# A fused attention and MLP kernel: batch 0 computed in whole tiles, and batch 2 loaded in transpose order by groups

## The chip, the cores and the metric

The kernel runs on one NeuronCore of a Trainium2 chip. Times are device microseconds (us) of one execution. A kernel is timed in several runs, on the same chip as the kernel before. The main number before the change is 419.73 us, median of 3 runs.

Five engines matter. TensorE (PE) multiplies matrices, ScalarE (ACT) does the exponentials, reciprocals and GELU, VectorE (DVE) adds and copies, GpSimd (POOL) issues all loads from DRAM that cast to fp16, and SyncE (SP) issues the stores and the transposing DMAs.

## The reference

```python
# q, k, v: (8 batches, 12 heads, 448 rows, 64), float32
scores = q @ k.T / sqrt(64)
m = max(scores)
e = exp(scores - m)
attn = e / (sum(e) + exp(-m) + 1e-9)         # "softmax off by one"
x = (attn @ v) laid out as (3584 tokens, 768)
h = x @ w_in                                  # 768 x 2048
out = gelu_exact(h) @ w_out                   # 2048 x 768
```

The kernel calls x @ w_in "layer 1" and the last product "layer 2".

## The kernel before

Twelve heads make three groups of four, so there are 24 groups numbered s = 0 to 23; batch b has groups 3b to 3b+2. Per group there are seven key chunks of scores, exponentials into `et`, the value products, and the denominators: VectorE sums the seven tiles into `ksum`, and four matmuls with a matrix of ones add that up.

q and k must be transposed for the scores. Batches 0 and 1 are turned by TensorE. From batch 2 on a transposing DMA does it, issued by SyncE. It needs its source in chunk order. For batch 2 VectorE makes that order; for batches 3 and up the load itself writes it, in short runs:

```python
def load_ordered(name, b):                    # POOL, one DMA per half, group and head pair
    for x in range(2):
        for g in range(NG):
            for e in range(2):
                nc.gpsimd.dma_start(out=by_chunks(name, b)[half[x], g, :, e, :], in_=dram(name, b)[x][:, g, e])

def order_and_turn(name, b, g):
    o = order_pool.tile([P, J, 2, D], FP16, name="order" + name)
    for e in range(2):
        nc.vector.tensor_copy(out=o[:, :, e, :], in_=natural(name, b)[:, g, e])
    nc.sync.dma_start_transpose(out=turned(name, b)[:, g], in_=o...)
```

Batch 0 goes through nine narrow passes (three slices of the queries by three groups), with narrow pieces of layer 1 between them; then come a burst of GELUs and the attention of batch 1 beside layer 2 of batch 0. At the end of that part stands this:

```python
    for name in "qk":
        alloc_raw(name, 3)
        nc.vector.memset(raw[name, 3][:, 0:1], 0.0)   # one column, on VectorE
        load_ordered(name, 3)                         # POOL: must wait for that memset
```

The memset writes into the tile that the load fills, so the load of batch 3 cannot be issued before VectorE comes to this place in its own program.

The steady cycle of a batch, cut:

```python
for b in range(1, B - 1):
    s = NG * (b + 1)
    values(s - 1); gap_after_values(s - 1, 2); next_three(s)
    ...            # 16 layer 1 chunks of batch b beside group s, with GELU
    ...            # loads of later batches
    s += 1; next_three(s); gap(3); last_one(s); gap(1 + b % 2); values(s); gap_after_values(s, 2 + b % 2)
    s += 1; next_three(s); gap(2); last_one(s); gap(2)       # gap: layer 2 items
```

In layer 2 of batch 0 the stores of the first half of the columns are kept back, because the second half of w_out comes late, and all go out with the first store of the second half:

```python
    if b == 0 and nh == 0:
        held.append(lambda: store([(nc.sync, osb, x, w)]))
    else:
        store([(nc.sync, osb, x, w)])
        for f in held:
            f()
```

The softmax here doesn't subtract the row's maximum and nothing guards it: scores larger than these inputs give would overflow.

Of the kernel before, what the change touches and what calls it, by code (L numbers as in the profile page):

```python
# [9 lines left out]
FP32 = mybir.dt.float32  # L10
# [9 lines left out]
def kernel(  # L20
# [14 lines left out]
    P = 128  # L35
# [7 lines left out]
    JA = 4  # L43
    NBURST = 8
# [16 lines left out]
    order_pool = ctx.enter_context(tc.tile_pool(name="order_pool", bufs=3))  # L61
# [56 lines left out]
    def load_ordered(name, b):  # L118
        if (name, b) not in raw:
            alloc_raw(name, b)  # L120
        for x in range(2):
            for g in range(NG):
                for e in range(2):
                    nc.gpsimd.dma_start(  # L124
                        out=by_chunks(name, b)[half[x], g, :, e, :], in_=dram(name, b)[x][:, g, e])
# [11 lines left out]
    def load_w_out(nh, i, n):  # L137
# [7 lines left out]
    PASS = [(0, 2, [(0, 4), (4, 7)]), (2, 4, [(0, 4), (4, 7)]),  # L145
            (4, 7, [(0, 2), (2, 4), (4, 6), (6, 7)])]
# [6 lines left out]
    KA = 4  # L153
    QF = PASS[0][1]
    pieces = (("q", 0, QF), ("k", 0, KA), ("k", KA, J))
# [12 lines left out]
    nc.gpsimd.memset(gt_even[:, 0:4, :], 0.0)  # L168
# [5 lines left out]
    for g in (1, 2):  # L174
        load_group("q", 0, g, 0, JA)
        load_group("k", 0, g)
        load_group("v", 0, g - 1)
    load_group("v", 0, 2)
    if QF < JA:
        load_group("q", 0, 0, QF, JA)  # L180
    load_all("q", 0, JA, J)
    for i in range(4):
        load_w_in(i, 4)
    load_group("q", 1, 0)
    load_group("k", 1, 0)
    for i in range(2):
        load_w_out(0, i, 2)
    load_group("q", 1, 1)
    load_group("k", 1, 1)
    load_all("v", 1)  # L190
    for i in range(2):
        load_w_out(1, i, 4)
    load_group("q", 1, 2)
    load_group("k", 1, 2)
    for i in range(2, 4):
        load_w_out(1, i, 4)
# [26 lines left out]
    def order_and_turn(name, b, g):  # L223
        o = order_pool.tile([P, J, 2, D], FP16, name="order" + name)
        for e in range(2):
            nc.vector.tensor_copy(out=o[:, :, e, :], in_=natural(name, b)[:, g, e])
        nc.sync.dma_start_transpose(
            out=turned(name, b)[:, g], in_=o.rearrange("p j e d -> p (j e d)"))
# [31 lines left out]
    def den_mms(dst, ksum):  # L260
        for x in range(2):
            for e in range(2):
                nc.tensor.matmul(  # L263
                    dst[half[e], x], ones[half[x]], ksum[half[x], e], start=True, stop=True)
# [22 lines left out]
    def exps(s, j, st):  # L287
        if j == 0:
            et_t[s] = et_pool.tile([P, J, 2, S], FP16, name="et")
            sum_t[s] = sum_pool.tile([P, 1024], FP16, name="ksum")  # L290
        et = et_t[s]
        exp_scores(et[:, j], st[:, :, 0:S])
        if j:
            ksum = sum_t[s][:, 0:2 * S].rearrange("p (e s) -> p e s", e=2)
            adds.append(lambda: add(ksum, et[:, 0] if j == 1 else ksum, et[:, j]))
# [5 lines left out]
    def values(s):  # L301
        val_t[s], den_t[s] = new_st(), new_st()
        st = new_st() if s + 1 < B * NG else None
        value_mms(val_t[s][:, :, 0:S], s, et_t.pop(s))
        den_mms(den_t[s][:, :, 0:S], sum_t.pop(s)[:, 0:2 * S].rearrange("p (e s) -> p e s", e=2))
# [123 lines left out]
    NUNIT = len(PASS) * NG  # L429
    QH = JA * D  # L430
    hv = {}

    def width(i):
        j0, j1, tiles = PASS[i // NG]
        return (j1 - j0) * D

    def h_scores(i, *ts):
        j0, j1, tiles = PASS[i // NG]
        n = width(i)
        made = []  # L440
        for t in ts:
            st = new_st()
            for jj, j in enumerate(range(*tiles[t])):
                score_mms(st[:, :, jj * n:(jj + 1) * n], i % NG, j, j0, j1)
            made.append((i, t, st))
        return made

    def h_exps(made):
        for i, t, st in made:
            n = width(i)  # L450
            k0, k1 = PASS[i // NG][2][t]
            if t == 0:
                et_t[i] = et_pool.tile([P, J, 2, S], FP16, name="et").rearrange(
                    "p j e s -> p (j e s)")[:, 0:J * 2 * n].rearrange(
                        "p (j e s) -> p j e s", j=J, e=2)
                sum_t[i] = sum_pool.tile([P, 1024], FP16, name="ksum")
            exp_scores(
                et_t[i][:, k0:k1].rearrange("p j e s -> p e j s"),
                st[:, :, 0:(k1 - k0) * n].rearrange("p e (j s) -> p e j s", j=k1 - k0))

    def h_sums(i, j):
        n = width(i)
        e = et_t[i].rearrange("p j e s -> p (j e s)")
        acc = sum_t[i][:, 0:4 * n]
        if j == 2:
            add(acc, e[:, 0:4 * n], e[:, 4 * n:8 * n])
        elif j == 4:
            add(acc, acc, e[:, 8 * n:12 * n])
            add(acc[:, 0:2 * n], acc[:, 0:2 * n], acc[:, 2 * n:4 * n])
        else:  # L470
            add(acc[:, 0:2 * n], acc[:, 0:2 * n], e[:, 12 * n:14 * n])

    def h_values(i):
        n = width(i)
        hv[i] = new_st()
        value_mms(hv[i][:, :, 0:n], i % NG, et_t.pop(i))
        den_mms(
            hv[i][:, :, QH:QH + n],
            sum_t.pop(i)[:, 0:2 * n].rearrange("p (e s) -> p e s", e=2))

    def h_reciprocal(i):
        n = width(i)
        rec_t[i] = rec_pool.tile([P, 2, S], FP32, name="rec")
        reciprocal(rec_t[i][:, :, 0:n], hv[i][:, :, QH:QH + n])

    def h_normalize(i):
        n, g, c0 = width(i), i % NG, PASS[i // NG][0] * D
        nc.vector.tensor_tensor(
            out=xt_of(0)[:, 2 * g:2 * g + 2, c0:c0 + n], in0=hv.pop(i)[:, :, 0:n],
            in1=rec_t.pop(i)[:, :, 0:n], op=ALU.mult)  # L490

    def h_layer1(f0, f1, c0, c1, w):
        ph = ps_bank.tile([P, 512 // w, w], FP32, name="bank")
        for f in range(f0, f1):
            for m in range(MCH):
                nc.tensor.matmul(  # L496
                    ph[:, f - f0, 0:c1 - c0], w_in_sb[:, m, f * P:(f + 1) * P],
                    xt_t[0][:, m, c0:c1], start=m == 0, stop=m == MCH - 1)
        return ph

    FPH = NBURST // 2 * S // QH
    QP = 2 * D

    def early1(pas, k):
        i, part = divmod(k, 2)
        f0, f1 = (0, FPH // 2 + 1) if part == 0 else (FPH // 2 + 1, FPH)
        ph = h_layer1(i * FPH + f0, i * FPH + f1, pas * QP, (pas + 1) * QP, QP)
        if (pas, part) == (0, 0):
            h_t[i] = h_pool.tile([P, NBURST // 2 * S], FP32, name=f"hbuf{i}")
        nc.vector.tensor_copy(  # L510
            out=h_t[i].rearrange("p (f s) -> p f s", s=QH)[:, f0:f1, pas * QP:(pas + 1) * QP],
            in_=ph[:, 0:f1 - f0])

    def window0():
        load_table(SET_GELU)
        for i in range(2):
            gelu(gt_even[:, i * FPH:(i + 1) * FPH, 0:QH],
                 h_t[i].rearrange("p (f s) -> p f s", s=QH))
        f0 = 2 * FPH
        gelu(gt_even[:, f0:, 0:QH], h_layer1(f0, FCH, 0, QH, QH))  # L520
        w = NFULL - QH
        for f in range(0, FCH, 2):
            if f in (8, 12):
                turn_on_pe("q" if f == 8 else "k", 1, 0)
            ph = h_layer1(f, f + 2, QH, S, QH)
            gelu(gt_even[:, f:f + 2, QH:], ph[:, :, 0:w])
            gelu(gt_odd[:, f:f + 2, 0:D], ph[:, :, w:w + D])
        load_table(SET_LN_EXP)
        l2.extend(layer2_items(0))


    nc.vector.tensor_copy(out=natural("q", 0)[:, 0, :, 0:QF, :], in_=first_rows["q", 0])
    nc.scalar.copy(out=natural("k", 0)[:, 0, :, 0:KA, :], in_=first_rows["k", 0])
    turn_on_pe("q", 0, 0, 0, QF)
    turn_on_pe("k", 0, 0, 0, KA, tile_=ps_st.tile([P, J, P], FP16, name="st"), copy=nc.scalar.copy)
    h_exps(h_scores(0, 0))
    nc.vector.tensor_copy(out=natural("k", 0)[:, 0, :, KA:J, :], in_=first_rows["k", KA])
    turn_on_pe("k", 0, 0, KA, J)
    h_exps(h_scores(0, 1))

    def turn_q(g, j0, j1):
        turn_on_pe("q", 0, g, j0, j1)

    def turn_qk(g):
        turn_q(g, 0, JA)
        turn_on_pe("k", 0, g)

    before1 = {
        0: lambda: turn_qk(1),
        1: lambda: turn_qk(2),  # L550
        2: lambda: turn_q(0, 2, JA),
        5: lambda: turn_q(0, JA, J),
    }
    after1 = {
        5: lambda: early1(0, 0),
        6: lambda: turn_q(1, JA, J),
        7: lambda: (turn_q(2, JA, J), early1(1, 0)),
        8: lambda: early1(0, 2),
    }
    after2 = {  # L560
# [193 lines left out]
```

## Time and profile before

| | before |
|---|---|
| median of 3 runs | 419.73 us (419.51 to 419.86) |
| span of the profiled run, mean granted clock | 419.3 us, 0.973 (this run, timed as the others are, took 421.03 us) |
| PE busy | 396.3 us (95%), 3835 matmuls |
| ACT, DVE, POOL busy | 274.4, 188.7, 139.3 us |

PE is busy 95% of the span, so it bounds the kernel as a whole. The prediction below shows where the other 5% and the low clock lie: in the first 90 us.

### The profile page before, as it was taken

What the parts mean: (1) busy time and instruction counts of PE and PEld (TensorE: products, weight loads), DVE (VectorE), ACT (ScalarE), POOL (GpSimd) and SP (SyncE); (2) the same over time, 40 slices, a digit from 0 to 9 for tenths busy, and PEclk for the clock granted to TensorE, in tenths of its full rate; (3) what the DMA queues carried; (4) which work ended last, traced back from release to release, by engine and by line L of the source; (5) the groups of instructions that cost most, each with busy time, mean ns of one, the idle gap of its engine ahead of it and who ended that gap; (6) DMA issues with size and microseconds to landing.
All of it is one profiled execution on the core that took longest, in us unless ns stands there. A gap on an engine that the chain in (4) does not pass through costs nothing.

```text
span 419.3 us, 9164 instructions
## 1 busy us (share of the span) xinstructions
PE 396.3 (95%) x3835; PEld 222.2 (53%) x3835; DVE 188.7 (45%) x339; ACT 274.4 (65%) x378; POOL 139.3 (33%) x209
## 2 busy tenths in 40 slices
PE   6768898889999999999999999999999999999995
PEld 3657774444555455554555455554555455555564
DVE  2747416786335650556335650556235650640021
ACT  4667757786777675867767776867776776854300
POOL 9913545029969968522930200020000000000000
PEclk8659999999999999999999999999999999999999
DMA  8999999269999999939972860149012100120032
GB/s 135 147 203 205 184 201 160 46 127 163 172 155 147 133 164 158 101 78 196 90 64 69 138 106 20 38 85 177 13 29 69 39 0 20 39 57 20 1 78 73
DMA packets 118377, 42.97 MB, mean 102 GB/s; under 512 B 92992, under 2 KB 118336, under 8 KB 118336
## 3 DMA queue, kind: packets, MB, share of 16 engines
q0 software_dynamic: 75424, 22.52, 51.6%
q1 hardware_dynamic: 42320, 19.52, 23.0%
q8 instruction: 30, 0.49, 0.5%
q10 hardware_dynamic: 592, 0.34, 0.3%
q14 instruction: 11, 0.09, 0.1%
HBM read 45.61 MB, written 11.01 MB: 135 GB/s over the span
## 4 chain that ended last, share of the span: by engine, by line
PE 87%; ACT 6%; DVE 2%; POOL 2%; issue 2%; DMA 1%; DVEq 0%; POOLq 0%
PE bank L380 34%; PE bank L340 31%; PE st L256 8%; PE st L247 8%; PE bank L496 4%; ACT et L267 2%; ACT gt_even L330 1%; PE st L263 1%; DMA rawk<-in_k_dram 1%; DVE ksum L270 1%; ACT rec L273 1%; PE bank L216 1%; ACT L69 1%; POOL rawq L106 1%; ACT rec L274 1%
## 5 line engine op out<-in xcount | busy, mean ns | idle before, releaser
L267 ACT ACTIVATE et<-st 128x896 f16<-128x896 f32 (+3 forms) x171 | 143.7, 901 | 35.2 <-PE st L247 35.0
L340 PE MATMUL bank<-xt,w_in_sb 128*128 128x448 f16 x672 | 130.9, 353 | 0.0
L270 DVE TENSOR_TENSOR ksum<-ksum,et 128x896 f16<-128x896 f16 (+2 forms) x123 | 72.3, 588 | 79.8 <-ACT et L267 76.9
L340 PEld LDWEIGHTS <-w_in_sb 128*128 128x128 f16 x672 | 64.3, 98 | 63.8 <-issue 5.9
L380 PE MATMUL bank<-w_out_sb,gt_odd 128*128 128x384 f16 (+1 forms) x528 | 87.0, 322 | 0.0
L380 PEld LDWEIGHTS <-gt_odd 128*128 128x128 f16 x528 | 49.7, 98 | 36.6 <-issue 6.4
L380 PE MATMUL bank<-w_out_sb,gt_even 128*128 128x384 f16 x384 | 66.7, 327 | 1.3 <-DVE tqk L217 1.3
L247 PE MATMUL st<-tqk 64*64 64x448 f16 (+2 forms) x840 | 49.1, 334 | 7.8 <-issue 2.5
L124 POOL DMA_DIRECT2D rawq<-in_q_dram x60 | 42.9, 722 | 37.5 <-issue 25.0
L399 DVE COPY osb<-bank 128x384 f32<-128x384 f32 (+1 forms) x56 | 30.7, 549 | 49.2 <-PE bank L380 49.2
L380 PEld LDWEIGHTS <-gt_even 128*128 128x128 f16 x384 | 35.6, 98 | 30.3 <-issue 7.4
L273 ACT ACTIVATE rec<-st 128x896 f32<-128x896 f32 (+2 forms) x30 | 23.0, 768 | 42.1 <-PE st L263 42.0
L114 POOL DMA_DIRECT2D rawv<-in_v_dram x28 | 17.4, 629 | 84.8 <-PE st L263 75.5
L256 PE MATMUL st<-et,rawv 64*64 64x448 f16 (+2 forms) x840 | 39.8, 330 | 4.1 <-ACT et L267 1.9
L124 POOL DMA_DIRECT2D rawk<-in_k_dram x60 | 42.6, 718 | 0.0
L330 ACT ACTIVATE gt_odd<-bank 128x448 f16<-128x448 f32 (+2 forms) x72 | 29.1, 405 | 18.3 <-PE bank L340 18.3
L350 DVE COPY hbuf<-bank 128x448 f32<-128x448 f32 x48 | 29.9, 623 | 22.7 <-PE bank L340 22.4
L247 PEld LDWEIGHTS <-tqk 64*64 64x64 f16 x840 | 20.9, 115 | 29.0 <-issue 19.4
L321 DVE TENSOR_TENSOR xt<-st,rec 128x896 f16<-128x896 f32 x21 | 22.8, 1086 | 24.5 <-ACT rec L274 24.5
L256 PEld LDWEIGHTS <-rawv 64*64 64x64 f16 x840 | 22.3, 116 | 19.6 <-issue 11.6
L330 ACT ACTIVATE gt_even<-bank 128x384 f16<-128x384 f32 (+2 forms) x33 | 15.3, 467 | 19.3 <-PE bank L340 14.3
L270 DVE TENSOR_TENSOR ksum<-et 128x896 f16<-128x896 f16 (+2 forms) x30 | 17.3, 577 | 21.9 <-ACT et L267 21.8
(44 smaller groups left out, 209.2 us busy)
## 6 DMA issues: line engine op xcount, KB each, us to landing
out_dram<-osb SPq DMA_DIRECT2D x110, 96.0 KB, 2.2
rawv<-in_v_dram POOLq DMA_DIRECT2D x28, 168.0 KB, 5.5
rawq<-in_q_dram POOLq DMA_DIRECT2D x60, 56.0 KB, 3.8
rawk<-in_k_dram POOLq DMA_DIRECT2D x60, 56.0 KB, 3.2
w_in_sb<-in_moe_w_in_dram POOLq DMA_DIRECT2D x4, 768.0 KB, 15.1
rawk<-in_k_dram POOLq DMA_DIRECT2D x16, 112.0 KB, 6.2
w_out_sb<-in_moe_w_out_dram POOLq DMA_DIRECT2D x2, 768.0 KB, 17.3
w_out_sb<-in_moe_w_out_dram POOLq DMA_DIRECT2D x4, 384.0 KB, 8.3
```

Of the source, the lines that this page charges most:

```text
L124: nc.gpsimd.dma_start(out=by_chunks(name, b)[half[x], g, :, e, :], in_=dram(name, b)[x][:, g, e])
L247: nc.tensor.matmul(dst[half[x], e], turned("k", b)[half[e], g, j, half[x]], turned("q", b)[half[e], g, j0:j1, half[x]], start=True, stop=True)
L256: nc.tensor.matmul(dst[half[e], x], natural("v", b)[half[x], g, e, j, :], et[half[x], j, e], start=j == 0, stop=j == J - 1)
L267: nc.scalar.activation(out=out, in_=st, func=AF.Exp, bias=-shift, scale=scale)
L270: nc.vector.tensor_tensor(out=out, in0=a, in1=x, op=ALU.add)
L273: nc.scalar.activation(out=rec, in_=den, func=AF.Ln, bias=math.exp(-shift), scale=1.0)
L321: nc.vector.tensor_tensor(out=xt_of(b)[:, 2 * g:2 * g + 2, :], in0=val_t.pop(s)[:, :, 0:S], in1=rec_t.pop(s), op=ALU.mult)
L330: nc.scalar.activation(out=out, in_=in_, func=AF.Gelu)
L340: nc.tensor.matmul(ph[:, 0:S], w_in_sb[:, m, fc * P:(fc + 1) * P], xt_t[b][:, m, :], start=m == 0, stop=m == MCH - 1)
L350: nc.vector.tensor_copy(out=h_t[i][:, n * S:(n + 1) * S], in_=ph[:, 0:S])
L380: nc.tensor.matmul(po[x][:, 0:w], gt[:, fc, g0:g0 + P], w_out_sb[:, fc, n0 + x:n0 + x + w], start=fc == 0, stop=fc == FCH - 1)
L399: nc.vector.tensor_copy(out=osb[:, 0:w], in_=po[x][:, 0:w])
```

## The change

The diff is shortened, and `...` marks cuts. Intent: do away with the narrow passes. Batch 0's first group runs in mixed tiles as its rows come in, its other two groups as whole tiles, and the steady cycle begins with batch 0, beside the attention of batch 1. Batch 2 comes in chunk order straight from DRAM, group by group, so that VectorE need not order it.

```diff
-    for i in range(NUNIT):                  # the nine narrow passes, 140 lines
-        ...
-    window0()
+    first_scores(0, 0)                      # group 0 by 2 key chunks and by query parts
+    ...
+    values(0); normalize(0); next_three(1); last_one(1)
+    values(1); normalize(1); next_three(2); last_one(2)
...
-    for b in range(1, B - 1):
+    for b in range(B - 1):
...
     def values(s):                          # for s < 3: denominators from all seven tiles
+            den_mms(den_t[s][:, :, 0:S], *(et[:, j] for j in range(J)))
+            value_mms(val_t[s][:, :, 0:S], s, et)
...
-    def order_and_turn(name, b, g):
+    def turn_ordered_group(name, b, g):     # transposing DMA straight from the loaded tile
...
+        if b == 0:                          # after layer 1 of batch 0
+            for name in "qk":
+                load_ordered(name, 2, [0])
+            load_w_out(1, 0, 2)
+            for name in "qk":
+                load_ordered(name, 2, [1])
+            load_w_out(1, 1, 2)
+            for name in "qk":
+                load_ordered(name, 2, [2])
+            load_all("v", 2)
...
         gap(1 + b % 2)
+        if b == 0: turn_ordered_group(q and k, 2, 0)
         values(s)
         gap_after_values(s, 2 + b % 2)
         s += 1
         next_three(s)
         gap(2)
+        if b == 0: turn_ordered_group(q and k, 2, 1)
         last_one(s)
         gap(2)
+        if b == 0:
+            turn_ordered_group(q and k, 2, 2)
+            for name in "qk":
+                load_ordered(name, 3)
-        alloc_raw(name, 3)
-        nc.vector.memset(raw[name, 3][:, 0:1], 0.0)
```

## The prediction

> **What bounds the kernel now.** I read the page's forty slices first, to see where TensorE is not full.
>
> ```profile
> PE   6768898889999999999999999999999999999995
> ACT  4667757786777675867767776867776776854300
> PEclk8659999999999999999999999999999999999999
> DMA  8999999269999999939972860149012100120032
> ```
>
> One slice is 10.5 us. From the tenth slice on PE shows 9 at a full clock; before that it shows 6 to 8, and the granted clock falls to 5 in the third slice. So there are two regimes: a start of some 90 us with holes, and a steady cycle that TensorE bounds. The change rewrites the start. The chain of waits, asked for 84 to 140 us, shows the border:
>
> ```profile
> 89.64 1.52 PE st L256 x28
> 91.15 0.21 PE st L263 x4
> 91.39 0.93 ACT rec L273
> 92.34 0.95 ACT rec L274
> 93.29 1.62 ACT et L267 x2
> ...
> 94.95 0.38 PE st L247 x4
> 95.34 2.38 PE bank L340 x12
> ...
> 102.61 13.72 PE bank L340 x72
> ...
> 137.06 1.45 PE st L256 x28
> ```
>
> Columns are start, duration and work. At 89.64 the value products of group 5 (batch 1's last) start: call it V5. From there both programs run the same code. V5 to V8 is one full cycle of 47.4 us (89.64 to 136.99 in the timeline), nearly all of it PE. Eight such cycles would be 379 us of the 419, so the start can give up at most some 35 to 40 us in all, and most of that is the loading and the first softmax, which nothing can hide. **The whole question is how much earlier V5 comes.**
>
> The groups, shapes kept apart, give the prices:
>
> ```profile
> L267 ACT ACTIVATE et<-st 128x896 f16<-128x896 f32 x147 | 125.2, 915 | 28.8 <-PE st L247 28.7
> L274 ACT ACTIVATE rec<-rec 128x896 f32<-128x896 f32 x21 | 19.9, 950 | 0.7
> L217 DVE COPY tqk<-bank 128x896 f16<-128x896 f16 x8 | 5.0, 622 | 10.5 <-PE bank L216 10.4
> ```
>
> An exponential of 896 columns costs 0.92 us alone and 0.85 in a row (three in 2.54 us in the timeline). In the chain a layer 1 chunk (6 matmuls) is 1.19 us of PE, a layer 2 item (8 matmuls) 1.355, 28 value products 1.45, the scores of one key chunk 0.23, 14 transposes 0.58.
>
> Last, the windows of the clock in the start (columns: stretch, then length, busy PE, PEld, DVE, ACT and POOL, clock, DMA share, GB/s):
>
> ```profile
> 11.26:14.67 3.41, 3.10 (x90) 2.55 (x82) 2.35 (x6) 1.73 (x2) 3.40 (x6) 0.50 1.26 169
> 14.67:18.08 3.41, 1.50 (x72) 1.15 (x68) 2.82 (x9) 3.10 (x6) 3.41 (x6) 1.00 1.06 114
> 18.08:21.50 3.42, 2.73 (x88) 2.23 (x85) 2.04 (x7) 2.91 (x5) 2.37 (x4) 0.50 1.09 163
> 28.30:31.70 3.40, 3.40 (x56) 3.20 (x56) 1.46 (x5) 1.71 (x3) 0.88 (x1) 0.50 1.24 208
> ```
>
> The clock changes at edges 3.41 us apart. A window with 1.5 us of PE work is followed by half clock, one with 3.1 or more by full clock, one with 2.7 at half clock stays there.
>
> **What the Trainium skill says.** "TensorE: Matmul & The Clock Gate", Part 1, has the same 3.4 us free-running window, half clock after an idle one and full after a busy one; the table above agrees, though 1.5 us of short matmuls were not enough to count as busy. "ScalarE: Activation LUTs", What ACT_TABLE_LOAD costs, gives about 1283 ns per table load; the trace has 1.28, and the change keeps the number of switches of batch 0 at two. "DMA: Bandwidth & Descriptors", SWDGE vs HWDGE vs iDMA, says that a cast during a DMA must be issued from GpSimd, so all loads that cast share one issuer: the trace has POOL at 9.99 us busy of 10 in the stretch 10 to 20.
>
> **The change, part by part.** *Removed:* the nine narrow passes over batch 0 with their 276 narrow layer 1 matmuls, the burst of GELUs at 46 to 60 us in which little else ran (ACT 4.98 of 10 us busy in the stretch 50 to 60), and the window after it, 60 to 90 us, in which batch 1's attention was mixed with layer 2 alone and PE still had gaps of 0.6 to 1.3 us. Also 12 ordering copies on VectorE (4.0 us, not on PE's path at all). *Added:* denominators of groups 0 to 2 from seven tiles, not one sum: 24 more matmuls each, 6 x 4 in 6/7 of 1.45 = 1.24 us. *Moved:* 16 layer 1 chunks of batch 0 beside group 3, layer 2 beside groups 4 and 5; two items (12 less 10) are still open at V5, against one before.
>
> *Start to the last exponential of group 0.* The first rows land about as before (same 384 KB ahead of the first scores), so the first exponential starts at about 6.8 (7.13 before). The next two wait: piece k[2:7] has 704 KB ahead of and with it (576 KB landed at 6.39 before), estimate 7.4; cast, transposes at half clock, copy and scores make 9.7. The third tile's scores stand behind the turning of q[4:7]: 10.8. Then they run in a row: 0.9, 0.45, 0.7 x 3, 0.45, and one small wait; the end is about **14.8**.
>
> *Groups 1 and 2.* ACT is the bound. Nine units per group: seven exponentials 7 x 0.85 = 5.95, two of the reciprocal 1.87, one hand-over 0.15: 8.0 us. PE needs only 1.6 + 1.45 + 1.45 + 2 x 0.58 = 5.7 of it at full clock. In group 0's hand-over VectorE copies a turned q ahead of the normalisation, whose score buffer the second tile of the next burst needs: +0.9. So exponentials end at 14.8 + 8.9 + 8.0 = 31.7 if the clock is full. It is hardly full at 14.8: the stretch 7.8 to 14.7 has small matmuls and waits. At half clock 28 + 28 products take 3.2 + 3.2, not 1.5 + 1.5, until the window after the 95% busy one: I put +1.8 on this. The end of group 2's exponentials, A2, is then **33.5**. Later, at 5.7 of 8 us (71%) busy, the clock may drop once more (+1.7) or never have been low.
>
> *A2 to V5.* Laid out in program order by the prices above. Value products, reciprocal and normalisation of group 2 end at A2 + 4.9. In the first eight chunks VectorE is in the way, as two turned copies (1.24), six sums (3.7) and the copies of 0.62 share two banks with PE: values of group 3 start at A2 + 12.3, where the steady cycle has 11.1. Eight more chunks with GELU straight from the bank end at A2 + 28.5. Then 3 scores, 28 transposes and 3 items, 3 scores, 1 item: values of group 4 at A2 + 36.8. Then 4 items, 6 scores and 2 items to V5 at **A2 + 48.2**. A check from the other side: 47.4, less 3 items (13 in a steady cycle, 10 here) 4.1, plus transposes 2.3 and the denominators 1.2, plus 1.3 of VectorE waits, gives 48.1.
>
> *Sum.* V5 at 33.5 + 48.2 = 81.7, against 89.6: 7.9 us earlier. After it there is one item more (1.36 us), which mostly fills PE gaps of 0.79 and 0.42 us that the timeline has at 93 to 95 us: +0.2. 419.7 - 7.9 + 0.2 = 412.0. Without any clock loss it is 410.2; with two it is 413.7.
>
> **Rivals.** *(1) The clock stays full.* The 28 + 28 contiguous products look made for that, and the stretch 74 to 80 us of before held full clock with PE at 4.2 of 6. About 410. *(2) Loads take over.* Up to the last quarter of w_in 7.1 MB (as stored) must land; before moved 6.8 MB by 40 us, so it lands at about 42, and is wanted at A2 + 24 = 57. The values of batch 1 (5.6 MB, about 35 us) are wanted at 46, its second q group (4.7 MB, 30 us) at 37. The second half of w_out stands behind ordered loads that POOL issues at 0.72 us for 56 KB: two groups are 16 of these, 11.5 us, so it should land by 65, and is wanted at about 75. All have 7 us or more. If the order costs what I do not see, 414 to 417. *(3) VectorE or ACT bounds the first cycle*, because layer 2 is missing as filler beside group 3, and the two banks stall: A2 + 50 and 414. *(4) The old narrow passes were worth it*, as they used PE while ACT worked: nothing gained, 418 to 420. Against it: PE was 65 to 71% busy in the first 30 us, much of it at half clock, and had four gaps of 1.1 to 2.5 us there.
>
> **Range and chances.** The sum is 412.0; rival 1 seems somewhat likelier than a second loss, so I take 411.5. Steps A (14.8) and the clock are each uncertain by 2 us, the cycle by 1.5, loads can only add: 407 to 416. Faster by over 2% means below 411.3, almost at my centre: 0.47; within 2% 0.50; slower 0.03.
>
> **What would show it.** Right: a first exponential at about 7, group 0's last at about 15; ACT without long gaps to A2 near 33; V5 near 82; PE full from A2 + 5 on, with short waits on VectorE's copies; the rest unchanged. Wrong: granted clock 1.0 throughout from 11 us (then A2 near 31.5), or 0.5 up to 35 us (A2 at 36); PE waiting for w_in, w_out, rawv or rawq transfers; values of group 3 later than A2 + 14; or a cycle after V5 unlike the old one, which I have assumed the same.

## The result and the profile after

The changed kernel took 415.45 us, median of 4 runs (413.73 to 416.25), against 419.62 us (419.13 to 419.86) for the kernel before, which now has a fourth run. The ratio is 0.9897, 95% interval 0.9864 to 0.9929: within 2%. Ratios here are the mean time of one kernel's runs over that of the other's of the same rounds, so they are not quite the ratio of the medians quoted. Executions over 1.5% slower than the fastest of the same kernel are left out of the means.

The time lies in the predicted range and 4 us above its centre. But the two halves of the sum came out quite differently from the prediction. The slices of the changed kernel:

```profile
PE   7878999949999999999999999999999999999995
ACT  4997776645775787777775786867775776844300
PEclk9999999978999999999999999999999999999999
DMA  8999999999999999759952930258012100220032
```

The granted clock is high from the first slice, in this run: the 5 and 6 of before are gone. PE is at 9 from the fifth slice on. Then there is a 4 in the ninth slice, 83 to 93 us, with the clock at 7 in it and 8 in the next, where the kernel before had 8 and then 9 at a full clock. This is the new hole. Windows of the start, laid 3.40 us long, show the same (columns as in the prediction's windows):

```profile
26.60:30.00 3.40, 2.16 (x34) 0.92 (x34) 1.13 (x2) 3.40 (x6) 2.54 (x4) 1.00 1.26 201
33.40:36.80 3.40, 1.90 (x39) 1.04 (x34) 3.02 (x5) 3.40 (x5) 0.65 (x1) 1.00 1.20 192
```

ACT is busy without a break in these, so it bounds groups 1 and 2, and the clock stays at 1.00 though PE has only about 2 us of work. The prices of the groups are the old ones: an exponential of 896 columns has a mean of 916 ns, now 161 of them, and a turned copy 622 ns, now 10.

The chain of waits from 70 to 135 us (start, duration, work) goes through it:

```profile
75.34 6.47 DMA rawv<-in_v_dram
81.81 9.26 DMA tqk<-rawk
...
91.11 0.96 PE st L236 x8
```

Before 91 us the chain is made of transfers and of POOL issuing them, and only after that of PE. In the sum by engine DMA is now 15% of the chain, where it had 1%:

```profile
PE 77%; DMA 15%; POOL 6%; issue 1%; DVE 0%; ACT 0%; POOLq 0%
```

The timeline of PE (start, duration, line, tiles, count; in brackets the idle time before it and what released it):

```profile
30.18 1.52 PE L253 MATMUL st<-et,ones 64*64 64x448 f16 x28 [0.43 <-ACT et L258]
...
77.30 1.52 PE L245 MATMUL st<-et,rawv 64*64 64x448 f16 x28
...
85.36 0.38 PE L236 MATMUL st<-tqk 64*64 64x448 f16 x4
91.11 0.96 PE L236 MATMUL st<-tqk 64*64 64x448 f16 x8 [5.37 <-DMA tqk<-rawk]
92.01 4.11 PE L340 MATMUL bank<-xt,w_in_sb 128*128 128x448 f16 x12
...
132.33 1.52 PE L245 MATMUL st<-et,rawv 64*64 64x448 f16 x28
```

At 30.18 the denominators of group 2 start, as soon as its last exponential is done (A2 of the prediction). At 77.30 stands V5, 12.3 us earlier than the 89.64 of before. At 85.36 PE does the first scores of group 7, and then waits 5.37 us for the turned k of that group. After the wait it runs at half clock: 12 layer 1 matmuls take 4.11 us, where the same 12 took 2.44 us at 82.99.

V8, the value products of group 8, start at 132.33, where before had 136.99. The cycle from V5 to V8 is thus 55.03 us long (132.33 - 77.30) against 47.35 (136.99 - 89.64): 7.68 us are given back. The wait is 5.37 of them, and the half clock in those 12 matmuls 1.67 (4.11 - 2.44). What the stall costs in all is seen in the versions below that have none after V5 (e2_turn_early, e3_no_hold, e5_early_gate and e6 to e9): there the same cycle takes 46.94 to 46.95 us, 0.40 less than in the kernel before in spite of the layer 2 item more. So the stall costs 8.08 us (55.03 - 46.95). The spans, 419.3 and 414.5, differ by 4.8, about what V8 is ahead: 4.7.

Why is the k of group 7 late? The queue of SyncE in the kernel after:

```profile
74.60 5.47 SPq L387 DMA_DIRECT2D out_dram<-osb  x8
80.24 1.41 SPq L216 DMA_TRANSPOSE tqk<-rawq  x1
81.81 2.39 SPq L216 DMA_TRANSPOSE tqk<-rawk  x1
```

and in the kernel before:

```profile
84.19 5.01 SPq L387 DMA_DIRECT2D out_dram<-osb  x8
89.30 2.04 SPq L227 DMA_TRANSPOSE tqk<-orderq  x1
91.44 1.25 SPq L227 DMA_TRANSPOSE tqk<-orderk  x1
```

In both kernels the two transposes of group 7 stand right behind a batch of eight stores, the held ones and those that released them. Before, k was issued at 91.44, and PE took it at 97.64 without a wait, so it had landed within 6.2 us. Here it is issued at 81.81 and lands at 91.07, 9.3 us later. The median landing times of the transposes in the stretches around them (first the kernel before, 72 to 102 us, then after, 60 to 90; the last number is us from issue to landing):

```profile
tqk<-orderk SPq DMA_TRANSPOSE x3, 3.3
```

```profile
tqk<-rawk SPq DMA_TRANSPOSE x2, 9.0
```

What else is under way at that time is seen on POOL. The ordered loads of batch 3, first the kernel before, then after:

```profile
90.86 0.77 POOL L124 DMA_DIRECT2D rawq<-in_q_dram  x1 [22.45 <-issue]
```

```profile
75.97 5.04 POOL L124 DMA_DIRECT2D rawq<-in_q_dram  x7
```

Before, POOL stood still for 22.45 us at the gate, and the loads began at 90.86, after the turning of group 7's q had been issued. The gate in VectorE's timeline of the kernel before:

```profile
90.26 0.06 DVE L648 MEMSET rawq<- 128x1 f16 x1
```

Now nothing holds them, and seven of them are issued before and around the transposes. "DMA: Bandwidth & Descriptors" of the Trainium skill, Issuing engines are not separate DMA queues, says that DMAs of the scalar, sync and gpsimd engines run on the same 16 DMA engines and interleave. The landing times agree: 3.3 us with the loads held, 9.0 us without. That is a comparison of few transposes (3 and 2) in kernels that differ in more than this; e1_gate3 below tests it.

### The profile page after: what moved, and what is told of

Read it like the earlier page. It is cut to its first block, busy times and chain, and to the rows that moved or that the text cites. A ratio compares the mean times of both kernels' runs of the same rounds, so it can differ in the third digit from the quotient of the medians.

```text
span 414.5 us, 8199 instructions
## 1 busy us (share of the span) xinstructions
PE 395.6 (95%) x3395; PEld 207.1 (50%) x3395; DVE 171.8 (41%) x281; ACT 271.8 (66%) x367; POOL 145.2 (35%) x213
## 4 chain that ended last, share of the span: by engine, by line
PE 77%; DMA 15%; POOL 6%; issue 1%; DVE 0%; ACT 0%; POOLq 0%
PE bank L380 32%; PE bank L340 31%; PE st L236 7%; PE st L245 6%; DMA w_out_sb<-in_moe_w_out_dram 4%; DMA rawq<-in_q_dram 4%; DMA w_in_sb<-in_moe_w_in_dram 3%; DMA tqk<-rawk 2%; DMA rawv<-in_v_dram 2%; POOL rawq L124 1%; POOL rawk L124 1%; PE st L253 1%; POOL rawq L106 1%; POOL rawk L106 1%; POOL w_in_sb L132 1%
## 5 line engine op out<-in xcount | busy, mean ns | idle before, releaser
L340 PE MATMUL bank<-xt,w_in_sb 128*128 128x448 f16 x768 | 151.2, 355 | 0.7 <-DVE tqk L209 0.7
L340 PEld LDWEIGHTS <-w_in_sb 128*128 128x128 f16 x768 | 74.0, 98 | 75.0 <-issue 9.6
L261 DVE TENSOR_TENSOR ksum<-ksum,et 128x896 f16<-128x896 f16 x105 | 65.4, 622 | 80.9 <-ACT et L258 78.7
L124 POOL DMA_DIRECT2D rawq<-in_q_dram x72 | 51.6, 723 | 28.8 <-DMA tqk<-rawq 17.4
L124 POOL DMA_DIRECT2D rawk<-in_k_dram x72 | 51.3, 719 | 16.0 <-DMA w_out_sb<-in_moe_w_out_dram 9.2
L264 ACT ACTIVATE rec<-st 128x896 f32<-128x896 f32 x24 | 22.0, 917 | 42.3 <-PE st L253 42.3
L350 DVE COPY hbuf<-bank 128x448 f32<-128x448 f32 x56 | 34.9, 623 | 33.9 <-PE bank L340 33.5
L330 ACT ACTIVATE gt_odd<-bank 128x448 f16<-128x448 f32 (+1 forms) x72 | 28.7, 399 | 18.2 <-PE bank L340 18.2
L245 PE MATMUL st<-et,rawv 64*64 64x448 f16 x672 | 36.4, 352 | 0.0
L330 ACT ACTIVATE gt_even<-bank 128x384 f16<-128x384 f32 x32 | 15.7, 491 | 16.6 <-PE bank L340 16.4
L265 ACT ACTIVATE rec<-rec 128x896 f32<-128x896 f32 x24 | 22.8, 950 | 0.8
```

The costliest lines, as they stand in the source:

```text
L245: nc.tensor.matmul(dst[half[e], x], natural("v", b)[half[x], g, e, j, :], et[half[x], j, e], start=j == 0, stop=j == J - 1)
L261: nc.vector.tensor_tensor(out=out, in0=a, in1=x, op=ALU.add)
L265: nc.scalar.activation(out=rec, in_=rec, func=AF.Exp, scale=-1.0)
L330: nc.scalar.activation(out=out, in_=in_, func=AF.Gelu)
L340: nc.tensor.matmul(ph[:, 0:S], w_in_sb[:, m, fc * P:(fc + 1) * P], xt_t[b][:, m, :], start=m == 0, stop=m == MCH - 1)
L350: nc.vector.tensor_copy(out=h_t[i][:, n * S:(n + 1) * S], in_=ph[:, 0:S])
```

## The experiments

Two things could thus make k late: its place behind the stores (theory A), and the loads of batch 3 (theory B). Further theories are about the denominators and the clock (C: the added products hold the clock up; D: they do not matter), and about what lies behind the first stall: that a whole stretch is bound by transfers, so that cures don't add and earlier delays are absorbed (E), or that the cures add (F), or that a version hardly differs from the one it is built on (G). The first four kernels ran on one chip, the next four on a second, the last three on a third, each time beside the kernel before; all gave correct results. One check holds for all of them: in the eight profiled runs without a stall after V5 (e2, e3, e5, both of e6, e7, e8, e9) the time of the run less its V5 is 330.84 to 330.90 us. In the changed kernel it is 338.95 and in the kernel before 331.39. Without that stall, then, V5 alone decides the time of a profiled run, and what the median cannot tell apart can be read from V5, run by run.

### Batch 3's loads behind the memset again (e1_gate3)

```diff
             for name in "qk":
+                alloc_raw(name, 3)
+                nc.vector.memset(raw[name, 3][:, 0:1], 0.0)
                 load_ordered(name, 3)
```

> The changed kernel, with the gate of the kernel before put back: a one-column memset on VectorE ahead of batch 3's loads, so that they start after 80 us and not at 76. Theory A (the turning of batch 2's group 1 is issued late because it stands behind eight held stores in SyncE's queue): the transposes are still issued at 80 to 84 us, and the stall of 5.4 us before the scores at 91 us shrinks by at most 2: 413 to 415. Theory B (the transposes land slowly, 9 us and not 4, because batch 3's loads fill the DMA rings): they land in about 4 us, the stall falls below 1.5 us and the half clock after it goes: about 409.

Measured: 411.1 us (409.98 to 412.94), ratio 0.9805 (0.9757 to 0.9854), so 2% faster or a little less. The timeline of PE:

```profile
87.27 0.57 PE L236 MATMUL st<-tqk 64*64 64x448 f16 x8 [1.67 <-DMA tqk<-rawk]
```

The loads now start at 82.02, k is issued at 81.41, hardly earlier than in the changed kernel, and lands about 5.8 us later, not 9.3. The wait falls from 5.37 to 1.67 us, and the half clock after it is gone (the next 12 matmuls take 2.44). From V5 to the value products of group 6 it is 12.72 us, where the changed kernel needs 18.75 (96.05 - 77.30) and e2_turn_early, without the stall, 10.67 (89.86 - 79.19). So the ungated loads make up 6.03 of the 8.08 us of the stall, 3.70 of waiting and 1.67 of half clock among them. The result lies between the two theories and nearer to B, whose landing of 4 us and wait below 1.5 were not quite reached. What makes the rest, this run alone does not show.

### Group 7's transposes issued ahead of the stores (e2_turn_early)

```diff
                 turn_ordered_group(name, 2, 0)
+            for name in "qk":
+                turn_ordered_group(name, 2, 1)
         values(s)
...
         gap(2)
-        if b == 0:
-            for name in "qk":
-                turn_ordered_group(name, 2, 1)
```

> The changed kernel, with the turning of batch 2's group 1 issued next to that of group 0, ahead of the held stores in SyncE's queue. Theory A: its loads have landed by about 68 us, so it is done by 75; no stall at 86 to 91 us, no half clock after it, 7 us back: 408 to 409.5. Theory B in its strict form (the transposes are slow wherever they stand): they still have 10 us more, so 408 to 410 too; what would contradict both is a stall that stays or moves to group 2's turning (412 or more).

Measured: 408.9 us (407.75 to 410.06), ratio 0.9739 (0.9688 to 0.979): faster. No wait is left at 86 us, although landing still takes 8.6 us and the loads are ungated. So an earlier issue cures the stall too; both theories had put that down, so it does not decide between them. PE's timeline has the value products of group 6 at 89.86:

```profile
89.86 1.52 PE L245 MATMUL st<-et,rawv 64*64 64x448 f16 x28
```

But there is a new wait, for the second half of w_out:

```profile
74.41 1.46 PE L380 MATMUL bank<-w_out_sb,gt_even 128*128 128x384 f16 x8 [2.70 <-DMA w_out_sb<-in_moe_w_out_dram]
```

It makes V5 79.19, later than the 77.30 of the changed kernel, and takes back part of what the cure gives. By the check above, the runs of 407.75 and 408.04 us must have had V5 near 77 (an estimate: the time less 330.9), so this wait is probably not in every run.

### The stores not held (e3_no_hold)

```diff
-                    if b == 0 and nh == 0:
+                    if False:
                         held.append(lambda: store([(nc.sync, osb, x, w)]))
```

> The changed kernel, with the stores of batch 0's first half columns issued at once instead of held until the first store of the other half. The transposes of group 1 keep their place in the program but no longer stand behind a burst of eight stores. Theory A: they are issued at about 75 to 77 us, before batch 3's loads are deep in the rings, and the stall falls below 2 us: 408 to 411. Theory B: batch 3's loads still start at 76 us, the transposes still land in 8 to 9 us, so a stall of 1 to 4 us stays: 411 to 414.

Measured: 416.33 us (414.96 to 417.84), ratio 0.9926 (0.9878 to 0.9974): the same as the changed kernel. Theory A had put it at 408 to 411 us and theory B at 411 to 414; both missed. The queue of SyncE shows why: four stores that no longer wait now stand ahead of the transposes of the group before (issued from 62.64 to 67.96). PE's timeline:

```profile
78.69 0.96 PE L236 MATMUL st<-tqk 64*64 64x448 f16 x8 [5.54 <-DMA tqk<-rawk]
```

The k of group 6 is issued at 70.34, lands 8.3 us later, and PE waits 5.54 us for it, 12 us earlier than PE's stall in the changed kernel. Half clock follows again (16 layer 2 matmuls take 4.60 us and not 2.77). The stall has moved by one group.

### Denominators of groups 1 and 2 summed on VectorE (e4_den_sum)

```diff
-            if s >= NG:
+            if s >= 1:
                 sum_t[s] = sum_pool.tile([P, 2 * S], FP16, name="ksum")
...
-        if s < NG:
+        if s < 1:
             den_t[s], val_t[s] = new_st(), new_st()
...
+    add_up()                 # the sums, after each part of groups 1 and 2
```

> The changed kernel, with the denominators of groups 1 and 2 from a sum of the seven tiles on VectorE, as in the steady cycle, in place of seven times four products with ones: 48 matmuls, 2.5 us, less on TensorE in a stretch where ScalarE is the bound. Theory C (those products keep the clock up): the granted clock falls to 0.5 somewhere between 20 and 37 us, and batch 0's first layer 1 chunk starts 1.5 to 3 us later than at 36.6: 417 to 418. Theory D (the 448-column products and scores hold the clock by themselves): the clock stays at 1.0, the first layer 1 chunk starts within 0.5 us of 36.6, and the time is within 1 us of the changed kernel.

Measured: 416.53 us (411.08 to 416.76), ratio 0.9899 (0.9828 to 0.9971): the same as the changed kernel. Three of the four runs took 416.51 to 416.76 us and one 411.08, which is not explained. In the profiled run the clock was at half from 8 to 18 us, and again for some 3 us each about 33 and 39 us, and layer 1 began at 40.09, not 36.61. The first of these stretches began before the edit takes effect (after about 16 us), so not all of the 3.5 us is the edit's. The wait for k shrank to 2.64 us instead, and V5 to the next value products took 15.19 us and not 18.75. So 3.5 us lost at the start cost 0.5 in the profiled run (416.76 against 416.25): the wait for the transfer absorbed the rest. The clock did as theory C had it, the time as theory D. Turned round, this suggests that beyond some point a gain at the start is worth nothing either.

### Both cures (e5_early_gate)

The edits of e1_gate3 and e2_turn_early together.

> The early turning and the gate together. The two runs alone left two different waits: the gate left 1.7 us for the turned k at 87 us, the early turning 2.7 us for the second half of w_out at 72 us. Theory E (one DMA stretch bounds the time from 60 to 90 us, and what is taken from one transfer shows as another's wait): the w_out wait stays at 1 to 3 us, since nothing ahead of it changes; no other wait; 407.5 to 409.5, as with the early turning alone. Theory F (the two fixes add): 405 to 407.

Measured: 409.1 us (408.19 to 409.94), ratio 0.9736 (0.9694 to 0.9778). That is the 0.9739 of e2_turn_early alone. PE still waits for w_out, 2.06 us, and V5 is at 78.84. The cures don't add, as theory E had put down (407.5 to 409.5): with the early turning alone the stall at 86 us is gone, and what then holds PE is the next transfer in the order of loads.

### Batch 2 in rows, ordered by VectorE as before (e6_natural2, e6_again)

This is e5_early_gate with batch 2 loaded as in the kernel before, and group 7 turned a little later:

```diff
     def turn_ordered_group(name, b, g):
+        o = order_pool.tile([P, J, 2, D], FP16, name="order" + name)
+        for e in range(2):
+            nc.vector.tensor_copy(out=o[:, :, e, :], in_=natural(name, b)[:, g, e])
         nc.sync.dma_start_transpose(
-            out=turned(name, b)[:, g], in_=by_chunks(name, b)[:, g].rearrange("p j e d -> p (j e d)"))
+            out=turned(name, b)[:, g], in_=o.rearrange("p j e d -> p (j e d)"))
...
-                load_ordered(name, 2, [g])
+                load_group(name, 2, g)
...
         gap_after_values(s, 2 + b % 2)
+        # the turning of group 7's q and k stands here
```

> As e5_early_gate, but batch 2 comes as in the kernel before: loaded by rows in its natural order, put in transpose order by two VectorE copies per group and tensor. GpSimd issues 12 loads of 0.6 us in place of 24 of 0.72, and the bytes go in runs of 896 in place of 128. Theory E, with the short runs of the ordered loads as the cause of the full rings: w_out lands before 68 us, no wait at 72 or 87, the value products of group 5 at about 76.3, time 405.5 to 407. Rival G (the bytes count, not the runs; or the copies delay VectorE and with it TensorE): within 1 us of e5_early_gate, or slower.

Measured: 408.2 us (406.59 to 409.3), ratio 0.9717 (0.9678 to 0.9757). The windows of 80 to 90 us (length; busy PE, PEld, DVE, ACT, POOL; clock; DMA share; GB/s), first the changed kernel, then this one:

```profile
80.00:90.00 10.00, 5.48 (x40) 2.50 (x38) 6.03 (x10) 5.21 (x6) 6.71 (x10) 0.93 1.81 165
```

```profile
80.00:90.00 10.00, 10.00 (x97) 4.70 (x95) 7.28 (x13) 7.07 (x10) 8.05 (x12) 1.00 1.61 137
```

PE is busy 10.00 of 10 us here, and so in each window from 60 to 100. No wait for a transfer is left. Of 40 us from 50 to 90 POOL is busy issuing 16.0, where the changed kernel needs 27.2, and the transposes of k land after 2.7 us. The waits are as theory E had them, and V5 is at 75.74 (76.3 expected), but its time, 405.5 to 407 us, was missed by 1.2; and the edit changes the number of loads, the length of their runs and the place of group 7's turning together, so it does not single out the short runs. The median is only 0.9 us below that of e5_early_gate, less than the spread of either, so whether the natural form gains in itself stays open.

A second measurement in five rounds:

> e6_natural2 once more, in the same rounds as e9_natural2_den_sum, as its yardstick and for a closer figure against the kernel before: 407 to 409, ratio 0.970 to 0.974.

408.1 us (407.27 to 409.33, 6 runs), ratio 0.9745 (0.9718 to 0.9773). Its interval does not touch that of the changed kernel, 0.9864 to 0.9929: this version beats both kernels (so do e2_turn_early, e5_early_gate and e8_early_w_out).

### Sums on VectorE where the stall is cured (e7_early_den_sum)

The edits of e2_turn_early and e4_den_sum together.

> The early turning with the denominators of groups 1 and 2 summed on VectorE. In the earlier run with these sums the clock fell to 0.5 at 32 to 35.5 and at 38 to 41 us and layer 1 began 3.5 us later, but the time did not change, because the later wait for the turned k absorbed it. Theory C with that reading: here, with less of the later wait left, the loss shows, 1.5 to 4 us over the early turning alone: 410.5 to 413. If the time is again that of the early turning alone (408 to 409.5), the transfers bound the start and not the clock.

Measured: 409.8 us (408.87 to 411.39), ratio 0.9762 (0.9722 to 0.9802). The 410.5 to 413 us that theory C had put down missed. Layer 1 began 1.5 us later than in e2_turn_early (37.48 against 35.94), but the wait for w_out was all but gone and V5 came at 77.97. In this run w_out landed at least 1.1 us earlier than in e2_turn_early, whose 2.70 us of waiting are thus partly a matter of the run. The two profiles, with V5 earlier in spite of the later start, don't show what the sums cost here.

### The second half of w_out earlier (e8_early_w_out)

The edit of e2_turn_early, and:

```diff
             load_w_out(1, 0, 2)
+            load_w_out(1, 1, 2)
             for name in "qk":
                 load_ordered(name, 2, [1])
-            load_w_out(1, 1, 2)
```

> The early turning, with the second half of w_out issued ahead of batch 2's second group (8 ordered loads of 0.72 us each come after it instead of before). Theory E in the form of mere order: w_out is there by 66 us, the wait of 2.7 us at 72 goes, the value products of group 5 start at 76.5 in place of 79.2; group 1's rows land some 5 us later, still before they are needed at 85: 405.5 to 407.5. If the transfers as a whole are the bound, the wait moves to a turned q or k (group 0 or 1) and the time stays at 408 to 409.5.

Measured: 408.57 us (407.89 to 409.44), ratio 0.973 (0.9696 to 0.9764), not to be told from e2_turn_early: the expected 405.5 to 407.5 us missed. The wait for w_out was gone and V5 came at 77.56, 1.6 us earlier than in e2_turn_early. In the profiled run a stretch at half clock in the start took 1.2 us (28 denominator products of group 2 in 2.77 us and not 1.52). That does not account for the missing gain: two other runs at a clock of 0.999 took 408.73 and 407.89 us. The two profiled runs do differ by the 1.6 us (408.40 against 410.06); it is the other runs of e2_turn_early, down to 407.75, that make the medians alike. So the order of w_out is worth at most what that wait costs in the runs that have it.

### Sums on VectorE without any transfer waits (e9_natural2_den_sum)

The edits of e6_natural2 and e4_den_sum together, where nothing later can absorb a delay.

> The clock question again, in the version whose trace has no wait for a transfer after 40 us: e6_natural2, with the denominators of groups 1 and 2 summed on VectorE. Theory C (the products with ones hold the clock): half clock in at least one window between 25 and 40 us in most runs, layer 1 1 to 3.5 us later, nothing to absorb it: 1 to 3.5 us slower than e6_natural2 in the same rounds. Theory D (they do not matter): within 0.7 us of it.

Measured: 410.62 us (408.4 to 412.22, 6 runs, five rounds), ratio 0.9796 (0.9762 to 0.983), against 0.9745 of e6_again in the same rounds: 0.5% or some 2 us slower. Here the loss at the start goes through to the end. Layer 1 begins at 38.13 and not 36.19, V5 comes at 79.35 and not 76.58, and the profiled runs differ by the same 2.78 us (410.24 against 407.46). All six runs had a clock of 0.975 to 0.992, of e6_again three of six had 1.000. The windows of e9_natural2_den_sum, columns as before:

```profile
26.40:29.80 3.40, 1.85 (x30) 0.89 (x30) 2.62 (x4) 3.40 (x6) 2.63 (x4) 0.97 1.26 201
29.80:33.20 3.40, 3.18 (x40) 1.66 (x38) 2.66 (x5) 2.54 (x4) 3.38 (x6) 0.53 1.25 205
```

and the first of them in e6_again, where full clock follows:

```profile
26.40:29.80 3.40, 2.21 (x38) 0.97 (x41) 0.91 (x2) 3.40 (x5) 2.69 (x4) 1.00 1.28 206
```

With the 24 more denominator matmuls this window has 2.21 us of PE work and the clock stays; without them it has 1.85 and the clock halves. These windows do not lie on the edges at which the clock changes. In e9 it changes at 29.57, 32.98, 36.40 and 39.81; laid on these edges, the windows before the two falls have 1.62 and 1.69 us of PE work, and the one from 22.75 to 26.16, which kept the clock, 2.04. In the changed kernel, laid back from the fall at 88.61, the emptiest between 20 and 40 us has 1.92. This is no fixed threshold: in e8_early_w_out, which has the added matmuls, the clock fell after a window with 1.78, and in e7_early_den_sum it stayed after one with 1.75. In this pair, then, the added matmuls, which the prediction counted as a cost of 1.24 us per group, are worth more than they cost. How much of the 2 us is the clock is not cleanly separated: PE also waits for VectorE's sum (0.53 us) and for ACT (0.83 and 1.40 us) at the hand-overs.

### Only batch 2 in rows (e10_natural_only)

The changed kernel with the loads and ordering copies of e6_natural2, but neither the gate nor the earlier turning.

> The changed kernel with that part alone undone that loads batch 2 in transpose order: batch 2 by rows, ordered by VectorE copies, at the same places in the program; batch 3's loads are not gated, and group 1's turning still stands behind the eight held stores. Theory E (short runs fill the rings): batch 3's loads start earlier, at about 62 us, and most of them are through when the transposes are issued at 80; the stall before group 7's scores falls from 5.4 to 0 to 2.5 us: 408.5 to 411. If the place in SyncE's queue were all, the stall stays above 4 us: 414 to 416.

Measured: 415.59 us (413.06 to 419.54, of which the 419.54 was slow; the median of the three fast runs is 415.14), ratio 0.9898 (0.9858 to 0.9938): the changed kernel's. The 408.5 to 411 us of theory E missed. PE's timeline:

```profile
90.38 0.57 PE L240 MATMUL st<-tqk 64*64 64x448 f16 x8 [3.95 <-DMA tqk<-orderk]
```

k is issued at 80.99, behind the held stores, and lands 9.4 us later, as in the changed kernel. The 12 layer 1 matmuls after it run at half clock (4.13 us). PE also waits 1.29 us for group 6's k at 75.23. V5 to the next value products takes 16.50 us, against 18.75. With fewer loads of its own, POOL ran through the ungated loads of batch 3 from 63.46 to 81.21. So the form in which batch 2 comes makes at most a small part of the stall (5.83 us of the 8.08 stay without it); the missing gate and the place in the queue make the most of it.

## Why the prediction was right or wrong

**The bound and the question: right, as far as they went.** PE bounded the steady cycle, and V5 was the place to look. It came at 77.30.

**Start to the last exponential of group 0: right.** Predicted 14.8; it ends at about 14.6, and the denominators of group 0 start at 14.75.

**The clock: wrong, in the good direction.** The sum had 1.8 us for half clock; in the profiled run it was full in every window up to 88 us (rival 1). e9_natural2_den_sum shows that the added matmuls have a part in it. It is in part the run's luck: in the profiles of e1, e2, e3 and e5, whose start is the same code, the clock was at half for 3.4 us between 8 and 13 us, without a later A2 (29.50 in e2_turn_early).

**Groups 1 and 2: mis-sized.** Predicted 8.9 and 8.0 us, together 16.9; with a clock never low they took about 7.6 and 7.9, 15.5 in all. The hand-over of 0.9 us did not show. A2 came at 30.1 and not 33.5: 0.2 from group 0, 1.8 from the clock, 1.4 from these terms.

**A2 to V5: right.** Predicted 48.2, measured 47.2 (77.30 less 30.1). V5 was thus 4.4 us earlier than the predicted 81.7: 3.4 up to A2 and 1.0 here.

**After V5: the step that failed.** "From there both programs run the same code", and the cycle after V5 was one "which I have assumed the same", with 0.2 us for one more item. It took 7.7 us more; without the stall it takes 0.4 less (46.95 against 47.35), so all of this is the stall. The code of the engines is nearly the same, but what is under way in the DMA engines is not. The change had dropped the memset that held batch 3's loads, and the prediction listed it nowhere among the parts removed. Among its signs of being wrong it did name a cycle unlike the old one, but no cause for it. It counted landing times only up to V5, and only of loads; of the transposing DMAs, whose queue and place it could have read in the trace, it said nothing. e1_gate3 shows 3.70 us of the wait and the 1.67 us of half clock to come from the loads, e2_turn_early that issuing ahead of the stores takes away the wait as well.

**Sum.** For the two profiled runs, 421.03 - 12.34 + 7.68 = 416.37, measured 416.25; on the median that the prediction starts from, 419.7 - 12.3 + 7.7 = 415.1, measured 415.45. (The profile of the kernel before is of a run 1.3 us above that median, which the prediction did not allow for.) Two errors of opposite sign, 4.4 us too pessimistic up to V5 and 7.5 us (7.7 less 0.2) too optimistic after it, left 3.1 us on the predicted 412.0. That the time fell into the range of 407 to 416 is luck: with the error after V5 alone it would have been 419.5.

**The rivals.** Rival 2, loads that take over at 414 to 417 us, is nearest: its time fits, and transfers did bound the stretch. Its mechanism was another: it named loads wanted before V5, and the only one of them that came just in time was the second half of w_out, for which it had reckoned 10 us to spare (65 against 75) and PE waited until 74.41 in e2_turn_early. Rival 3 did not occur: A2 to V5 was no longer than predicted. Rival 4 is refuted by V5 itself.

**What stays open.** Whether the natural form of batch 2 gains in itself once both cures are in; how much of e9's loss is the clock; and how the stall that the gate leaves in e1_gate3 divides between the queue and the loads that still run.

## What to carry to other kernels

When a start is made shorter, everything that was timed against its end has to be checked again: ask of each transfer in the first cycle after it when it is issued, behind what it stands in its queue, and what else fills the DMA engines then. A line that looks like housekeeping, such as a memset of one column, can be the gate that keeps a later load out of the way; find what waits for it before you drop it. And where a transfer ends a stage, gains and losses ahead of it can vanish in the wait, so that the worth of an edit can only be read in a version without that wait.

## What the Trainium skill lacked or had wrong

- "DMA: Bandwidth & Descriptors", Latency and other measured facts, gives rates for the transposing DMA (261 GB/s, contiguous 350 to 400), but not what one takes beside loads. A turning of 128 x 896 fp16 elements (229 KB) landed after 2.7 to 3.4 us here with few loads under way and after 8.2 to 9.4 us beside loads in short runs (9.0 in the changed kernel; 8.2 and 8.6 in e5_early_gate, beside those of batch 2).
- No page that I read warns that a transposing DMA waits in its issuing queue behind the stores there: eight stores took 5.47 us to issue, and the transposes came right after them.
- "TensorE: Matmul & The Clock Gate", Part 1, says that half clock comes after an idle window. Here, with windows of 3.41 us laid on the edges at which the clock changes, it came between 20 and 40 us after windows with 1.62 to 1.78 us of PE work (e4, e7, e8, e9) and stayed away after ones with 1.75 to 2.16, so the border is not sharp. Other work behaves otherwise: 1.55 us of layer 2 tiles kept the clock (e2, 70.15 to 73.56), 2.06 us of small matmuls did not (e1, 5.75 to 9.16). A wait of 5.37 us cost 1.67 us more through the clock in the next 12 matmuls, one of 3.95 (e10) 1.69, those of 2.70 (e2) and 1.67 (e1) nothing.
